# Six parameter matrices: loaded plain and transposed on TensorE, or transposed by the load itself, with another order of all operations

## The chip, the cores and the metric

The kernel runs on one core of a Trainium2 chip. TensorE (PE) multiplies matrices, VectorE (DVE) and ScalarE (ACT) work on tiles, GpSimd (POOL) does small work and adds in transfers, SyncE (SP) mostly issues transfers (DMA). The metric is the device time of one execution in microseconds (us), the median of several runs.

## The reference, cut to what matters

The input is normalised, then an S4 state space convolution and a gated feed-forward layer are applied to it, and both are added to the input.

```python
L, D, N, F = 2048, 512, 128, 1792
def _A_ref(u, A_re, A_im, B_re, B_im, C_re, C_im, log_dt, Dskip):
    dt = jnp.exp(log_dt)[:, None]
    A, Bc, Cc = A_re + 1j * A_im, B_re + 1j * B_im, C_re + 1j * C_im   # each (512, 128)
    logdA, dB = dt * A, dt * Bc
    P = jnp.exp(logdA[:, :, None] * l[None, None, :])                  # l = 0 .. 2047
    K = jnp.einsum("dn,dnl,dn->dl", Cc, P, dB).real                    # (512, 2048)
    # y = causal convolution of u with K along the sequence, through FFTs of length 4096
    return y + u * Dskip

def _B_ref(x, w_gate, w_up, w_down):
    h = sigmoid(x @ w_gate) * (x @ w_up)
    return h @ w_down

xn = layernorm(A_u)
return A_u + _A_ref(xn, ...) + _B_ref(xn, w_gate, w_up, w_down)
```

The kernel builds K from powers of exp(dt A), which VectorE and ScalarE make by a ladder of squarings and products; TensorE does the transforms and the feed-forward layer.

## The kernel before: the parts concerned

Every operation is added to a plan, `pl.add(engine, cost, function, what it needs, ...)`, and numbered in order of adding. A list of numbers, `ORDER`, says in what order the operations are written into the program; each engine runs its own in that order. The waits between engines come from a tracker that looks at which parts of which tile an instruction reads and writes. Transfers take eight semaphores in turn, so that a transfer also waits for the one eight places before it. The costs are the planner's estimates and do nothing on the chip.

```python
# loads; names are those of the plan, "Are" is the real part of A
for qi, (nm, src) in enumerate([("Are", A_A_re), ("Aim", A_A_im), ("Bre", A_B_re), ("Bim", A_B_im),
                                ("Cre", A_C_re), ("Cim", A_C_im)]):
    rawn[nm] = at(OFF["G"] + qi * KB, [D])
    l_par[nm] = load("SP", rawn[nm], src.rearrange("(p k) n -> p (k n)", k=KT), 128 * KB, pkt=1024)
    if qi == 1:
        l_ld = load("SP", ld, A_log_dt.partition_broadcast(128), 128 * KB, pkt=1024)
        l_id = load("SP", ident[:], cten["ident"].ap(), 32 * KB)
# ... w_gate in three pieces, w_up in two, x in five, w_down in one

def keep_warm(n, prio):                       # idle matmuls, results unused
    def fn():
        for _ in range(n):
            T.matmul(bank(wsl), glu_sb[:, 0, 0:128], glu_sb[:, 0, :], start=True, stop=True)
    return pl.add("PE", 0.2155 * n, fn, (), prio, acq=[wsl], rel=[wsl])
warm = [keep_warm(n, -10) for n in (12, 8, 8)]
for n in range(3):
    keep_warm(5, -9 + n)

# layernorm of x, then xn to xnT: the first 512 rows by TensorE (line 573) and ScalarE (line 578),
# the others through DRAM with Y.dma_start_transpose (line 586)

# parameters: transposed on TensorE into PSUM (line 598) and read from there with a permutation
for nm in "ABC":
    def fp(nm=nm):
        for c in range(2):
            for t in range(4):
                T.transpose(bankb(tsl[nm])[:, 512 * c + 128 * t:512 * c + 128 * t + 128],
                            rawn[nm + ("re", "im")[c]][:, 128 * t:128 * t + 128], ident[:])
    pt_op[nm] = [pl.add("PE", 0.6, fp, [l_par[nm + "re"], l_par[nm + "im"], l_id], 5, acq=[tsl[nm]])]
def raw(nm, c):
    return bankb(tsl[nm])[:, 512 * c:512 * c + 512].rearrange("p (k q) -> p q k", k=KT)
# dt = exp(log_dt) on ScalarE (line 622), z = dt * A on VectorE (line 624), range reduction,
# exp and sin on ScalarE (lines 629 to 641), then the ladder of powers (lines 674 to 688)

# gate and up projection of a group of 512 rows: TensorE (lines 1034, 1049) into PSUM banks;
# sigmoid on ScalarE (line 1043); the product on VectorE (line 1064), reading the up projection
# from PSUM, or, for the units named in UEV, from a copy that ScalarE makes (line 1060)

# spectrum: for each of two halves p of the channels and eight groups u, matmuls of lines 903, 921
# and 944, evictions of lines 908, 923 and 948, and a store of 256 KB to v_scr[p]

# last transform: v comes back in eight loads of 256 KB for each half p
vall = at(0, [NP, 8, 2, 2, DW])               # [p, t, j, r, 256], 16 KB in each partition for each p
for t in range(8):
    for p in range(NP):
        lds.append(dma("SP" if p == 0 or t % 2 == 0 else "ACT", vall[:, p, t], v_v[:, :, 2 * t:2 * t + 2, :], ...))

def s2_mm(t, r, o, start, ps=(0, 1)):         # lines 1002 and 1004; row i = 2 t + r
    for j in range(2):
        T.matmul(o[:, w], s2[:, j, :], vall[:, ps[0]:ps[-1] + 1, t, j, r, :], ...)
    if i >= 12:
        T.matmul(o[:, w], sr[:, i - 12, :], rr[:, w], ...)
# for t = 0 .. 5 the result goes to VectorE (line 1017), is added and stored as 256 KB of the output;
# rows 12 to 15 (t = 6 and 7) come on top of the down projection of the last group (lines 1082, 1099)
```

Of the kernel before, what the change touches and what calls it, by code (L numbers as in the profile page):

```python
# [14 lines left out]
ALU = mybir.AluOpType  # L15
# [160 lines left out]
def _consts():  # L176
# [30 lines left out]
UEV = (15, 17, 19, 23, 24, 25, 28, 30, 32, 33, 34, 35, 36, 37, 38, 39, 41, 42, 47)  # L207
ON_ACT = (0, 2)
ORDER = [
    1, 0, 3, 2, 39, 40, 5, 4, 23, 26, 8, 30, 29, 52, 41, 42, 31, 43, 33, 49, 32, 53, 55, 54, 57, 44, 56, 45, 46, 34, 25, 24,  # L210
    47, 6, 9, 14, 12, 19, 10, 35, 58, 36, 37, 125, 98, 59, 100, 48, 97, 7, 38, 142, 649, 63, 650, 651, 99, 65, 11, 15, 660,
    17, 637, 638, 51, 64, 113, 661, 112, 126, 66, 643, 101, 639, 67, 68, 50, 644, 645, 102, 103, 60, 680, 136, 681, 69, 655,
    656, 70, 690, 61, 691, 700, 701, 20, 13, 16, 665, 124, 104, 666, 695, 696, 685, 705, 670, 105, 686, 706, 137, 123, 671,
    702, 71, 62, 127, 662, 682, 683, 703, 663, 106, 138, 111, 72, 704, 110, 107, 108, 128, 697, 664, 148, 646, 115, 143,
    684, 698, 109, 707, 699, 129, 114, 74, 647, 708, 709, 648, 73, 640, 151, 692, 75, 693, 672, 641, 149, 76, 232, 185, 673,
    642, 77, 687, 27, 674, 694, 233, 116, 186, 675, 78, 79, 132, 676, 688, 145, 652, 677, 80, 689, 234, 187, 22, 150, 678,
    82, 144, 21, 81, 130, 667, 152, 668, 188, 679, 18, 146, 653, 654, 669, 83, 786, 657, 788, 178, 84, 658, 659, 85, 147,
    153, 787, 235, 86, 88, 710, 120, 711, 789, 791, 154, 87, 179, 792, 155, 793, 712, 156, 180, 236, 189, 190, 756, 139,
    191, 237, 89, 790, 90, 91, 713, 238, 92, 93, 118, 794, 140, 192, 95, 194, 184, 141, 172, 718, 766, 163, 173, 195, 133,
    719, 795, 203, 204, 181, 205, 197, 117, 174, 182, 198, 196, 193, 207, 720, 206, 208, 209, 211, 183, 761, 767, 757, 212,  # L220
    131, 762, 169, 726, 768, 728, 727, 170, 213, 160, 164, 214, 729, 215, 134, 200, 769, 119, 730, 770, 736, 746, 748, 216,
    166, 171, 737, 219, 749, 747, 165, 771, 121, 758, 210, 217, 750, 759, 167, 763, 772, 161, 218, 764, 220, 221, 760, 168,
    162, 765, 175, 738, 222, 94, 741, 753, 157, 201, 199, 96, 739, 176, 202, 158, 740, 778, 742, 779, 721, 223, 224, 122,
    135, 225, 239, 754, 227, 242, 751, 240, 250, 251, 244, 752, 776, 252, 159, 177, 733, 249, 254, 243, 755, 777, 255, 253,
    731, 780, 734, 245, 256, 743, 781, 258, 744, 259, 745, 782, 260, 732, 226, 773, 854, 783, 735, 247, 774, 228, 279, 722,
    241, 261, 407, 377, 775, 784, 262, 852, 378, 785, 229, 379, 280, 263, 281, 266, 230, 264, 855, 853, 437, 231, 265, 246,
    248, 268, 796, 938, 408, 376, 380, 383, 438, 267, 797, 257, 269, 282, 439, 409, 270, 798, 283, 271, 799, 284, 272, 413,
    273, 274, 275, 326, 856, 285, 834, 444, 443, 286, 440, 289, 276, 290, 295, 277, 297, 287, 298, 441, 384, 442, 278, 410,
    382, 804, 299, 301, 445, 844, 300, 302, 800, 288, 305, 327, 303, 306, 381, 411, 414, 474, 412, 446, 447, 328, 385, 805,
    386, 448, 387, 806, 449, 296, 392, 291, 292, 845, 835, 939, 294, 307, 450, 415, 388, 416, 308, 842, 417, 393, 843, 389,  # L230
    812, 832, 309, 310, 394, 399, 418, 833, 313, 390, 311, 314, 451, 467, 400, 857, 401, 312, 419, 315, 858, 329, 395, 396,
    452, 398, 397, 504, 836, 330, 316, 468, 304, 317, 469, 420, 459, 470, 473, 421, 824, 862, 475, 813, 825, 331, 453, 837,
    318, 822, 454, 293, 472, 471, 457, 489, 319, 476, 456, 863, 321, 320, 823, 838, 336, 846, 402, 332, 458, 455, 403, 333,
    864, 404, 322, 341, 344, 477, 460, 337, 807, 865, 866, 345, 478, 859, 867, 405, 461, 826, 348, 462, 346, 860, 422, 423,
    391, 479, 429, 482, 839, 349, 943, 424, 428, 426, 425, 868, 480, 347, 944, 840, 352, 872, 817, 350, 861, 463, 353, 351,
    714, 339, 338, 427, 483, 354, 869, 430, 484, 818, 342, 431, 340, 406, 512, 847, 464, 848, 870, 488, 465, 490, 432, 871,
    355, 491, 873, 356, 485, 487, 877, 433, 827, 513, 486, 514, 878, 879, 323, 434, 564, 481, 497, 324, 828, 435, 814, 829,
    492, 357, 493, 358, 494, 815, 466, 360, 830, 841, 557, 436, 516, 519, 359, 334, 362, 363, 361, 880, 849, 874, 343, 875,
    495, 881, 498, 364, 496, 325, 850, 819, 365, 518, 808, 335, 558, 499, 820, 559, 366, 367, 816, 368, 876, 821, 831, 851,
    900, 502, 515, 517, 369, 370, 371, 882, 372, 505, 560, 503, 621, 563, 501, 520, 883, 506, 884, 629, 562, 500, 561, 631,  # L240
    901, 521, 507, 885, 579, 549, 508, 509, 565, 510, 522, 602, 890, 566, 603, 523, 524, 604, 940, 542, 609, 373, 374, 511,
    941, 891, 898, 543, 567, 525, 568, 572, 550, 928, 544, 551, 610, 942, 903, 569, 611, 573, 607, 605, 570, 574, 892, 899,
    929, 904, 606, 608, 580, 612, 958, 933, 613, 526, 547, 594, 581, 545, 546, 548, 534, 614, 527, 552, 528, 553, 893, 959,
    633, 576, 578, 587, 908, 945, 529, 615, 577, 535, 946, 909, 934, 588, 589, 536, 575, 582, 947, 571, 918, 948, 949, 554,
    919, 583, 584, 635, 905, 920, 555, 906, 907, 533, 595, 530, 531, 616, 532, 585, 596, 537, 375, 894, 921, 922, 925, 963,
    953, 926, 590, 538, 964, 591, 593, 592, 597, 598, 902, 539, 886, 599, 954, 556, 586, 923, 540, 913, 617, 935, 627, 623,
    600, 541, 936, 924, 914, 601, 625, 968, 955, 956, 960, 618, 937, 957, 626, 961, 915, 962, 624, 916, 917, 930, 910, 622,
    911, 931, 965, 932, 912, 950, 619, 634, 951, 632, 927, 636, 966, 620, 967, 952, 969, 801, 723, 724, 972, 802, 725, 973,
    970, 803, 715, 628, 630, 971, 895, 974, 716, 975, 976, 809, 977, 896, 717, 887, 810, 888, 897, 980, 978, 889, 811, 981,
    982, 979, 983, 984, 985, 28, 986]  # L250
# [60 lines left out]
def kernel(  # L311
# [39 lines left out]
    def bankb(slot):  # L351
        return bank(slot).bitcast(BF)
# [88 lines left out]
    for qi, (nm, src) in enumerate([("Are", A_A_re), ("Aim", A_A_im), ("Bre", A_B_re), ("Bim", A_B_im),  # L441
                                    ("Cre", A_C_re), ("Cim", A_C_im)]):
        rawn[nm] = at(OFF["G"] + qi * KB, [D])
        lp[0] += 0.01
        l_par[nm] = load("SP", rawn[nm], src.rearrange("(p k) n -> p (k n)", k=KT), 128 * KB, pkt=1024)
        if qi == 1:
            ld = at(OFF["G"] + 6 * KB, [D])
            l_ld = load("SP", ld, A_log_dt.partition_broadcast(128), 128 * KB, pkt=1024)
            l_id = load("SP", ident[:], cten["ident"].ap(), 32 * KB)
# [82 lines left out]
    warm = [keep_warm(n, -10) for n in (12, 8, 8)]  # L532
# [59 lines left out]
    tsl = {nm: _Slot(b) for nm, b in (("A", "gu"), ("B", "gu"), ("C", "po"))}  # L592
    pt_op = {}
    for nm in "ABC":
        def fp(nm=nm):
            for c in range(2):
                for t in range(4):
                    T.transpose(bankb(tsl[nm])[:, 512 * c + 128 * t:512 * c + 128 * t + 128],
                                rawn[nm + ("re", "im")[c]][:, 128 * t:128 * t + 128], ident[:])
        pt_op[nm] = [pl.add("PE", 0.6, fp, [l_par[nm + "re"], l_par[nm + "im"], l_id], 5, acq=[tsl[nm]])]  # L600

    def raw(nm, c):
        return bankb(tsl[nm])[:, 512 * c:512 * c + 512].rearrange("p (k q) -> p q k", k=KT)
# [16 lines left out]
    perm = lambda v: v.rearrange("p (q k) -> p q k", k=KT)  # L620
# [5 lines left out]
    q1 = pl.add("DVE", 0.60, lambda: tt(perm(pt_["z_im"]), raw("A", 1), perm(dtb), ALU.mult), [o_dt] + pt_op["A"], PR)  # L626
    q2 = pl.add("DVE", 0.60, lambda: tt(perm(pt_["z_re"]), raw("A", 0), perm(dtb), ALU.mult), [q1], PR, rel=[tsl["A"]])
# [24 lines left out]
    def f_g():  # L652
        tt(perm(pt_["db_re"]), raw("B", 0), perm(dtb), ALU.mult)
        tt(perm(pt_["db_im"]), raw("B", 1), perm(dtb), ALU.mult)
    qb = pl.add("DVE", 1.27, f_g, [o_dt] + pt_op["B"], PR + 2, rel=[tsl["B"]])

    def f_g2():
        tt(perm(pt_["t1"]), raw("C", 0), perm(pt_["db_re"]), ALU.mult)
# [494 lines left out]
```

## Time and profile before

| | |
|---|---|
| Time, median of 3 runs | 246.35 us (246.32 to 246.81) |
| Span of the profiled execution | 244.9 us |
| TensorE busy | 230.0 us (94%), 2070 matmuls in the records |
| VectorE busy | 187.6 us (77%) |
| ScalarE busy | 180.4 us (74%) |
| Idle matmuls (line 529) | 43, 11.9 us |
| Transposes of the parameters (line 598) | 24, in three groups of 0.61 us |
| Moved by DMA | 43.60 MB, mean 178 GB/s |

The profile is one execution in time. Busy shares are averages over the whole span, and this kernel has stages with different limits, so it is read stage by stage: which engine is full, and which wait ends last. In the lines shown further down, L12 is line 12 of the kernel, "big" is one large tile that holds most of the buffers, x8 is the number of instructions, and brackets name the idle time before an instruction and what ended it. "PEclk" or the clock in a table of stages is the granted clock of TensorE, 1.00 at full speed.

### The profile page before, as it was taken

The page shows a single profiled execution, that of the slowest core. Times are in us where ns is not written, and L with a number is a line of the kernel's source. Part 1 is how long each engine was busy: PE and PEld are TensorE (multiplying, and loading weights), DVE is VectorE, ACT ScalarE, POOL GpSimd, SP SyncE. Part 2 cuts the span into 40 slices and gives each one's busy share as a digit, 9 for nine tenths or more (in the row PEclk, how much of TensorE's full clock was granted, in tenths as well). Part 3 has the DMA queues.
Part 4 walks back from the last instruction along what each step waited for, and adds up shares of the span by engine and source line. Part 5 has one row for each costly group of instructions (what it writes and reads, how often), then busy time and mean ns, then how long its engine had stood idle before and what let it go on. Part 6 is the DMA issues. An engine that isn't in the chain of part 4 may idle for free.

```text
span 244.9 us, 5395 instructions
## 1 busy us (share of the span) xinstructions
PE 230.0 (94%) x2070; PEld 116.8 (48%) x2098; DVE 187.6 (77%) x397; ACT 180.4 (74%) x293; POOL 17.4 (7%) x42
## 2 busy tenths in 40 slices
PE   7959999899999999999999999999999999987695
PEld 2526444344444644555556555465555454433242
DVE  3899999999999999999999999923415345816232
ACT  5899999999999999659899999945577877000000
POOL 1202350000000200120000200000000200000000
PEclk9979999999999999999999999999999999999589
DMA  6999537122256964298376867636958987843403
GB/s 170 302 376 357 208 119 183 60 86 86 87 188 202 250 135 139 82 210 231 88 212 187 212 157 223 178 88 188 287 139 231 191 231 222 237 152 120 155 24 129
DMA packets 48459, 43.60 MB, mean 178 GB/s; under 512 B 9393, under 2 KB 41650, under 8 KB 48434
## 3 DMA queue, kind: packets, MB, share of 16 engines
q1 hardware_dynamic: 46338, 40.58, 55.9%
q0 software_dynamic: 864, 1.57, 4.1%
q10 hardware_dynamic: 1232, 1.11, 1.5%
q8 instruction: 16, 0.26, 0.5%
q14 instruction: 9, 0.07, 0.1%
HBM read 25.43 MB, written 12.06 MB: 153 GB/s over the span
## 4 chain that ended last, share of the span: by engine, by line
PE 41%; ACT 37%; DMA 9%; DVE 6%; issue 4%; SPq 1%; ACTq 0%
PE bank L1082 13%; PE bank L1034 6%; ACT hT_sb L1043 6%; PE pair L921 5%; DMA big<-v_scr 5%; ACT big L674 5%; PE bank L1049 4%; ACT big L705 4%; PE pair L828 3%; PE pair L944 3%; ACT big L557 3%; ACT sq_sb L796 3%; ACT big L680 2%; PE pair L1002 2%; ACT big L948 2%
## 5 line engine op out<-in xcount | busy, mean ns | idle before, releaser
L1034 PE MATMUL bank<-xnT,wg_sb 128*128 128x512 bf16 (+1 forms) x227 | 55.4, 377 | 2.3 <-ACT xnT L578 0.5
L1049 PE MATMUL bank<-xnT,wu_sb 128*128 128x512 bf16 x218 | 53.0, 379 | 1.0 <-issue 0.3
L1082 PE MATMUL bank<-wd_sb,hT_sb 128*128 128x512 bf16 x215 | 51.7, 389 | 1.1 <-issue 0.5
L1034 PEld LDWEIGHTS <-wg_sb 128*128 128x128 bf16 x236 | 23.0, 100 | 27.0 <-issue 5.1
L1082 PEld LDWEIGHTS <-hT_sb 128*128 128x128 bf16 x224 | 22.1, 100 | 27.5 <-issue 4.2
L1043 ACT ACTIVATE hT_sb<-bank 128x512 bf16<-128x512 f32 x56 | 32.8, 612 | 1.5 <-PE bank L1034 1.5
L1049 PEld LDWEIGHTS <-wu_sb 128*128 128x128 bf16 x224 | 20.9, 98 | 25.6 <-issue 2.5
L927 DVE TENSOR_TENSOR big<-big 128x2048 bf16<-128x2048 bf16 x16 | 19.5, 1216 | 17.8 <-DMA big<-big 11.2
L1064 DVE TENSOR_TENSOR hT_sb<-hT_sb,bank 128x512 bf16<-128x512 bf16 x37 | 24.3, 682 | 6.5 <-PE bank L1049 6.1
L739 DVE TENSOR_TENSOR big<-big 128x1024 bf16<-128x1024 bf16 (+4 forms) x40 | 25.7, 643 | 0.4
L740 DVE TENSOR_TENSOR big<-big 128x1024 bf16<-128x1024 bf16 (+4 forms) x40 | 25.7, 641 | 0.0
L921 PE MATMUL pair<-big 128*128 128x256 bf16 x160 | 20.0, 273 | 0.0
L908 ACT ACTIVATE big<-pair 128x1024 bf16<-128x1024 f32 x16 | 16.5, 1035 | 4.2 <-DMA big<-c_SR 2.3
L923 ACT ACTIVATE big<-pair 128x1024 bf16<-128x1024 f32 x16 | 16.4, 1026 | 3.2 <-PE pair L921 2.1
L948 ACT ACTIVATE big<-pair 128x1024 bf16<-128x1024 f32 x16 | 16.5, 1037 | 2.5 <-DMA v_scr<-big 1.4
L921 PEld LDWEIGHTS <-big 128*128 128x128 bf16 x160 | 15.3, 98 | 4.8 <-issue 1.0
L744 DVE TENSOR_TENSOR big<-big 128x512 bf16<-128x512 bf16 (+4 forms) x40 | 16.8, 419 | 0.2
L745 DVE TENSOR_TENSOR big<-big 128x512 bf16<-128x512 bf16 (+4 forms) x40 | 16.7, 417 | 0.0
L705 ACT ACTIVATE big<-pair 128x1024 bf16<-128x1024 f32 x16 | 16.3, 1042 | 0.0
L796 ACT ACTIVATE sq_sb<-big 128x256 bf16<-128x256 bf16 (+2 forms) x20 | 12.9, 650 | 2.5 <-DVE big L745 2.4
L674 ACT ACTIVATE big<-big 128x512 bf16<-128x512 f32 x24 | 13.9, 637 | 0.0
L529 PE MATMUL bank<-glu_sb 128*128 128x512 bf16 x43 | 11.9, 433 | 1.4 <-POOL glu_sb L522 1.4
(109 smaller groups left out, 276.8 us busy)
## 6 DMA issues: line engine op xcount, KB each, us to landing
big<-c_E SPq DMA_DIRECT2D x16, 320.0 KB, 3.9
z_scr<-big SPq DMA_DIRECT2D x16, 256.0 KB, 2.5
big<-z_scr SPq DMA_DIRECT2D x16, 256.0 KB, 3.6
big<-big SPq DMA_DIRECT2D x64, 64.0 KB, 3.1
v_scr<-big SPq DMA_DIRECT2D x16, 256.0 KB, 3.0
big<-v_scr SPq DMA_DIRECT2D x12, 256.0 KB, 4.3
big<-in_A_u_dram SPq DMA_DIRECT2D x4, 512.0 KB, 5.5
wd_sb<-in_B_w_down_dram SPq DMA_DIRECT2D x1, 1792.0 KB, 14.3
```

The costliest lines, as they stand in the source:

```text
L674: S.activation(out=W[p][:, k], in_=cur[:, :, DW * p:DW * p + DW], func=ACT.Identity)
L705: ev = pl.add("ACT", 0.90, lambda sl=sl, zs=zs: S.activation(out=zs().rearrange("p j d -> p (j d)"), in_=two(sl), func=ACT.Identity), [fx_ ...
L739: V.tensor_tensor(out=wide(outp), in0=wide(lo), in1=mre, op=ALU.mult)
L740: V.tensor_tensor(out=wide(tb()), in0=wide(lo), in1=mim, op=ALU.mult)
L796: a = pl.add("ACT", 0.11 + 0.213 * nn, lambda: S.activation(out=sq().rearrange("p r k c h -> p r k (c h)"), in_=src.rearrange("p r k c h - ...
L921: T.matmul(two(sk)[:, o:o + DW], es()[:, g, kt, :], kT[p][:, kt, :], start=kt in (0, NKT - 1), stop=kt >= NKT - 2)
L948: ev = pl.add("ACT", 0.90, lambda sv=sv, vs=vs: S.activation(out=vs().rearrange("p g y d -> p (g y d)"), in_=two(sv), func=ACT.Identity), ...
L1034: T.matmul(bank(sl)[:, c0:c1], w[:, kt, k * 128:(k + 1) * 128], xnT[:, grp, kt, c0:c1], start=(kt == 0), stop=(kt == KT - 1))
L1043: S.activation(out=hT_sb[:, hs.idx, k % 2, :], in_=bank(sl), func=ACT.Sigmoid)
L1049: T.matmul(bank(sl), wu_sb[:, kt, k * 128:(k + 1) * 128], xnT[:, grp, kt, :], start=(kt == 0), stop=(kt == KT - 1))
L1064: V.tensor_tensor(out=h(), in0=h(), in1=us_sb[:, us.idx, :] if on else bank(sl), op=ALU.mult)
L1082: T.matmul(bank(po), hT_sb[:, hts[k // 2].idx, k % 2, jj * 128:(jj + 1) * 128], wd_sb[:, k, :], start=(k == 0), stop=k == FT - 1, **kw)
```

## The change

The six parameter matrices, each 512 x 128 and 128 KB, are no longer loaded in plain form, transposed on TensorE and read from PSUM with a permutation. Each load transposes, the matrices land in SBUF in the form that the products need, and VectorE reads them there. This is meant to free TensorE and two PSUM banks early in the kernel and to leave the products without a permutation. The idle matmuls of the start, three blocks of 12, 8 and 8, become one of 28. Last, the order of all operations is another one, made with slack for transfers that come late, and another set of up projections (20 instead of 19) is copied by ScalarE.

```diff
-UEV = (15, 17, 19, 23, 24, 25, 28, 30, 32, 33, 34, 35, 36, 37, 38, 39, 41, 42, 47)
+UEV = (18, 19, 27, 28, 29, 30, 31, 32, 33, 34, 35, 36, 37, 38, 39, 40, 41, 44, 45, 52)
 ORDER = [          # cut to its end
-    ... 617, 935, 627, 623, 600, 541, 936, 924, 914, 601, 625, 968, 955, 956, 960, 618, 937, 957, 626, 961,
-    915, 962, 624, 916, 917, 930, 910, 622, 911, 931, 965, 932, 912, 950, 619, 634, 951, 632, 927, 636, 966,
-    620, 967, 952, 969, 801, 723, 724, 972, 802, 725, 973, 970, 803, 715, 628, 630, 971, 895, 974, 716, 975,
-    976, 809, 977, 896, 717, 887, 810, 888, 897, 980, 978, 889, 811, 981, 982, 979, 983, 984, 985, 28, 986]
+    ... 613, 936, 627, 629, 617, 947, 907, 932, 960, 937, 952, 614, 961, 619, 962, 964, 890, 623, 615, 891,
+    967, 965, 710, 625, 892, 711, 966, 631, 712, 621, 968, 969, 804, 718, 805, 971, 719, 806, 970, 972, 882,
+    883, 796, 975, 720, 797, 884, 798, 973, 976, 978, 974, 979, 977, 980, 981]
@@ loads of the six matrices
-        l_par[nm] = load("SP", rawn[nm], src.rearrange("(p k) n -> p (k n)", k=KT), 128 * KB, pkt=1024)
+        l_par[nm] = pl.add("SP", 1.27, lambda src=src, dst=rawn[nm]: Y.dma_start_transpose(dst, src), (), lp[0] + ...,
+                           dma=(128 * KB, _rate(256), 0.5))
@@ idle matmuls
-    warm = [keep_warm(n, -10) for n in (12, 8, 8)]
+    warm = [keep_warm(28, -10)]
@@ parameters
-    tsl = {nm: _Slot(b) for nm, b in (("A", "gu"), ("B", "gu"), ("C", "po"))}
-    for nm in "ABC":
-        def fp(nm=nm): ...                    # eight transposes on TensorE, as above
-        pt_op[nm] = [pl.add("PE", 0.6, fp, [l_par[nm + "re"], l_par[nm + "im"], l_id], 5, acq=[tsl[nm]])]
+    pt_op = {nm: [l_par[nm + "re"], l_par[nm + "im"]] for nm in "ABC"}
     def raw(nm, c):
-        return bankb(tsl[nm])[:, 512 * c:512 * c + 512].rearrange("p (k q) -> p q k", k=KT)
+        return rawn[nm + ("re", "im")[c]]
@@ the eight products with the parameters, one of them
-    q1 = pl.add("DVE", 0.60, lambda: tt(perm(pt_["z_im"]), raw("A", 1), perm(dtb), ALU.mult), [o_dt] + pt_op["A"], PR)
+    q1 = pl.add("DVE", 0.60, lambda: tt(pt_["z_im"], raw("A", 1), dtb, ALU.mult), [o_dt] + pt_op["A"], PR)
```

Five operations fewer are added, so a number above 46 after the change means the operation that was five higher before. The two ends, read with the names of the operations:

| | before | after |
|---|---|---|
| SyncE at first | x, x, A im, A re, identity, log_dt, C re, B re, C im, x, S1, x, w_gate 1, B im, w_gate 2, w_gate 3, x, w_down, w_up 1, w_up 2 | x, x, log_dt, A re, A im, identity, S1, x, w_gate 1, B im, B re, x, w_gate 3, x, w_gate 2, C re, SW, C im, Dskip, w_up 2, w_up 1, two stores of z, w_down |
| TensorE at first | 12 + 5 idle, transposes of A, 8 + 8 idle, transposes of xn, S1, gate units 2, 4, 0, transposes of C, gate 1, transposes of B, ... | 28 + 5 + 5 idle, transposes of xn, 5 idle, S1, gate units 2, 0, 10, S1, gate units 12, 8, 9, ... |
| Five idle matmuls | one group in the middle of the first group of rows, one after the last matmul | none there |
| Gate and up groups after the last product of half 1 | ten | seven |
| The end, on all engines | loads of half 1 for t=2, 1, 0, 6, 5, 7; down product of row 12; t=2; t=1; down product of row 13; row 13; row 12; t=0; loads of half 1 for t=3 and t=4; t=5; ... | loads of half 1 for t=5, 6, 0, 1; down product of row 12; t=5; load for t=3; down product of row 13; row 12; t=0; load for t=4; store of t=5; load for t=7; store of t=0; load for t=2; row 13; t=3; t=1; ... |

## The prediction

> **What bounds the kernel now.** I read the page first, then a table of busy time by stage, then the first 24 us in order of time, then the chain of waits from 200 us on and what the queue of SyncE waited for there. The span is 244.9 us. By stage (columns: stretch, length, busy time and instructions of PE, weight loads, DVE, ACT, POOL, granted clock, DMA share, GB/s):
>
> ```profile
> 15.00:30.00 15.00, 14.04 (x80) 7.74 (x81) 14.30 (x32) 14.94 (x27) 4.06 (x6) 0.89 0.92 317
> 130.00:150.00 20.00, 19.68 (x263) 11.13 (x266) 19.98 (x38) 19.55 (x35) 1.24 (x3) 1.00 0.70 175
> 150.00:205.00 55.00, 54.27 (x661) 29.63 (x668) 28.23 (x48) 39.12 (x54) 2.28 (x3) 1.00 0.75 202
> 205.00:218.00 13.00, 12.28 (x64) 5.34 (x65) 6.41 (x15) 2.87 (x5) 0.00 (x0) 1.00 0.74 223
> 218.00:230.00 12.00, 8.77 (x37) 3.64 (x38) 4.78 (x5) 0.00 (x0) 0.00 (x0) 0.88 0.40 135
> ```
>
> From 15 to 150 us TensorE, VectorE and, but for a stretch around 100, ScalarE are all busy; from 150 to 205 TensorE alone is full (54.27 of 55). So a stage gives time back only at the two ends. The start, in order of time:
>
> ```profile
> 3.08 0.43 SPq L417 DMA_DIRECT2D big<-in_A_log_dt_dram  x1
> 7.75 1.29 DVE L624 TENSOR_TENSOR big<-bank,big 128x512 f32<-128x512 bf16 x2
> 13.48 1.92 ACT L578 ACTIVATE xnT<-pair 128x1024 bf16<-128x1024 bf16 x2
> 14.54 0.38 PE L703 MATMUL pair<-big 128*128 128x512 bf16 x1 [2.14 <-ACT xnT L578]
> 15.45 4.45 PE L1034 MATMUL bank<-xnT,wg_sb 128*128 128x256 bf16 x20 [0.54 <-ACT xnT L578]
> ```
>
> The chain is: log_dt lands (7.1), exp, dt times A on VectorE (7.75), range reduction, exp and sin on ScalarE until 13.48, only then the eviction of the transposed xn, and the first gate matmul at 15.45. TensorE, whose last transposes ended at 12.39, stood still for 2.1 us, and the granted clock was 0.50 from 16 to 18 us.
>
> The end, first the chain, then a wait of SyncE's queue:
>
> ```profile
> 209.31 8.71 DMA big<-v_scr
> 218.03 1.89 PE pair L1002 x8
> 219.92 3.02 PE bank L1082 x14
> ...
> 224.05 4.20 DMA big<-v_scr
> 228.30 1.89 PE pair L1002 x4
> 230.19 1.71 PE bank L1082 x4
> ```
>
> ```profile
> SPq L417 <- PE bank L1004: 1.4, 1, 1.4
> ```
>
> Six of the eight loads of the second half of v arrive by 218.0. The last two (t=3, t=4) are issued at 224.05, just as the matmuls of row 12 end: in the program they wait for these. The reason is the shape of the read. `vall[:, 0:2, t, j, r, :]` takes 512 bytes from the first half and 512 bytes 16 KB further on; the program's dependency tracking treats everything between as read, so loads for other t, listed later, wait for it, and reads listed after those loads wait for them. TensorE stood 3.2 us (225.1 to 228.3) and the clock was then 0.50 until 234. A matmul of 512 columns starts every 0.43 us there and every 0.216 us before, so some 14 matmuls cost about 2.9 us more.
>
> **What the Trainium skill says.** "TensorE: Matmul & The Clock Gate", section "Why this matters for your kernels", advises no PE-idle gaps over about 3 us between matmul bursts, or the clock falls to half. The trace agrees in kind, and here gaps of 2.1 us (start) and 3.2 us (end) were followed by 0.50, while 0.6 us at 217.4 was not. "Advanced Engine Details and Errata", section "X-Bar Transpose (TRN2)", says that transposing DMAs are as fast as regular ones. In landing, about: the three of 512 KB took 4.4 to 5.4 us, plain loads of 512 KB took 5.5 (median). In issuing, no:
>
> ```profile
> L586 SPq DMA_TRANSPOSE xnT<-x_scr x3: 2080/2225/2520, 37.4 to 80.2; - x3
> ```
>
> against 0.43 us for a plain load. "VectorE: DVE Perf Modes", section "Why PSUM operands drop a tier", says that fp32 with a PSUM operand runs at 1x. The eight products here take 0.683 us with PSUM input and fp32 output; products of fp32 in SBUF (line 648) take 0.66, so I expect almost nothing from the move to SBUF.
>
> **The change part by part.**
> 1. TensorE loses 24 transposes of the parameters. Eight ended at 7.6 us, in idle time; the other 16 lie between 19.6 and 21.2 us and cost 2 x 0.61 = 1.2 us of a full engine.
> 2. The idle matmuls stay 43. Before, one group of five runs inside the full stretch (5 x 0.216 = 1.1 us), and five come after the last real matmul. After, 28 + 5 + 5 run at first and five right behind the transposes of xn. That takes 1.1 us out of the full stretch. From 1.43 us on, 17 matmuls took 5.75 us before; 21 more at 0.216 bring after's first 38 to about 11.7 us, just when xn is ready; the last five then cover one of the two idle microseconds, so the half clock after 15.45 may go: seven starts of 0.43 against 0.216, up to 1.6 us.
> 3. The start of the chain. log_dt is issued third, at about 1.65 instead of 3.08, and with its 4.0 us lands near 5.6. The two A transposes follow it. I estimate 1.1 us of issue each (the trace's 2.2 for four times the size, of which part must be fixed), so the second is issued by 4.3 and lands 2.2 to 2.9 us later, near 6.9. The product can start about 0.8 us sooner than 7.75, and the first gate matmul with it, near 14.7. It is not certain: ScalarE now does exp between two rows of statistics.
> 4. The four B and C transposes hold SyncE's queue 4 x (1.1 - 0.43) = 2.7 us longer ahead of weights and x. w_down (1.75 MB) however goes behind both w_up, which takes about 5 us of transfers (at 350 GB/s) out of their way. After's third gate unit already needs the last piece of w_gate, two units sooner than I would like, near 17 us: a stall up to 1 us.
> 5. VectorE: unchanged, but for 20 instead of 19 evictions of the up projection taken over by ScalarE (0.49 us each there, 0.68 down to 0.42 here).
> 6. The order. Up to the first table product (c=0) both lists have nearly the same TensorE work ahead, and so again at c=1 to c=3. After has 3 us more of VectorE work listed ahead of c=0 and none more at c=1, so I count the middle as neutral, with 2 us of doubt.
> 7. The end. After the last product of the second half (end T; 204.8 before) after has seven gate and up groups left before the first final matmul, not ten: 7 x 0.86 + 0.75 + 3.1 = about 10.2 us of filler for a wait that took 13.2 us with six loads. After needs only four loads for t=5, 0.5 MB less, at 0.23 MB/us some 2.2 us less: ready near T + 10.9. Idle 0.7, as before. Then t=5, the down product of row 13's block (3.0), row 12 of t=6, t=0: T + 16. Now row 13 is listed behind the loads of t=4 and t=2, and overlaps both by the shape above. The load of t=4 may go when row 12 is done. The load of t=2 stands in SyncE's queue behind the store of t=0, which waits for t=0's matmuls (0.9) and its addition (1.23); then two issues (1.0) and a landing of about 3. Together 6.2 us after row 12, of which t=0 covers 0.9: TensorE idles about 5.3 us instead of 3.2. The half clock follows as before. Cost: +2.1 us.
>
> Sum: of 1.2 + 1.1 + 1.6 + 0.8 = 4.7 us at the start I count 2, since VectorE is full until 150 us and does not get shorter; late transfers +0.6; the end +2.1. That is +0.7: 246.35 + 0.7 = 247.0 us.
>
> **The rivals.**
> The start wins in full (TensorE is the bound from 150 us on, and whatever it did sooner is not left for then): -4.7 + 2.1 gives 243.7. For it speaks 54.27 of 55 us; against it VectorE's 19.98 of 20 between 130 and 150.
> The transposing loads are late: if each takes as long to issue as the large ones (2.2 us), the second A lands at about 9, the chain starts 1.3 us later than before and the weights some 7 us later, with PE waits at a half clock: 250 to 252. For it speaks that issue time hardly varies (2.08 to 2.52); against it the planner's own cost in the diff, 1.27.
> The end is better than I read: if the load of t=2 isn't tied up behind the store, the gap stays under 3 us and perhaps the clock stays full: 2 to 5 us less, 242 to 245.
> The order's slack pays: TensorE's idle time between 15 and 205 us, 4.4 us now, halves: 245.
>
> **Range and chances.** The rivals lie from 242 to 252, most of them within 3 us of 247. Two per cent is 4.9 us. Eight in ten: 243.5 to 251. Faster by over 2% (under 241.4) needs the full start and a cured end together: 0.06. Slower by over 2% (over 251.3) needs late transposes or a stall in the middle: 0.10. The rest, 0.84, within.
>
> **What would show it.** The first gate matmul near 14.7 with the clock at 1.00 shows steps 2 and 3; a DMA_TRANSPOSE of the parameters at 0.9 to 1.3 us of issue shows step 4; a wait of TensorE on v_scr of about 5 us before row 13, followed by 0.50, shows step 7. I am wrong if the first gate matmul comes after 16, if TensorE idles over 6 us between 15 and 205, or if there is no such wait at the end.

## The result, and the profile after

The kernel after takes 249.72 us (median of 4 runs, 249.01 to 250.49) where the kernel before took 246.50 beside it (4 runs, 246.32 to 246.81): a ratio of 1.013, with a 95% interval of 1.0091 to 1.0169. That is inside the predicted range, within the 2%, and 2.7 us above the predicted 247.0. So the change costs 3.2 us where 0.7 was expected, and it is the sum and not only its size that has to be explained: the start came out at least as well as predicted, the wait at the end came out as predicted, and in between something was lost.

The table by stage of the kernel after (the columns as in the prediction: stretch, length, then busy time and instructions of PE, weight loads, DVE, ACT and POOL, granted clock, DMA share, GB/s):

```profile
15.00:30.00 15.00, 13.81 (x72) 6.82 (x72) 13.66 (x33) 14.16 (x27) 4.95 (x9) 1.00 0.98 307
150.00:205.00 55.00, 52.86 (x638) 28.61 (x645) 28.13 (x48) 39.21 (x54) 2.24 (x3) 1.00 0.72 194
205.00:218.00 13.00, 11.14 (x80) 4.80 (x70) 6.79 (x16) 3.24 (x5) 0.00 (x0) 1.00 0.77 215
218.00:230.00 12.00, 5.78 (x26) 2.42 (x27) 3.05 (x3) 0.59 (x1) 0.00 (x0) 0.86 0.45 132
```

At the start the clock is 1.00 instead of 0.89. From 150 us on TensorE has holes that the kernel before does not have: 2.1 us from 150 to 205 (before 0.7), 1.9 from 205 to 218 (before 0.7), 6.2 from 218 to 230 (before 3.2). Part of what looks like a hole, in both, is a matmul without a record: there are 2070 matmuls to 2098 weight loads before and 2045 to 2074 after.

The start in order of time (start, us, engine or queue, operation; idle time before it and its releaser in brackets):

```profile
2.13 1.23 SPq L445 DMA_TRANSPOSE big<-in_A_A_re_dram  x1
...
6.45 1.30 DVE L616 TENSOR_TENSOR big<-big 128x512 f32<-128x512 bf16 x2
...
14.16 1.91 PE L1026 MATMUL bank<-xnT,wg_sb 128*128 128x256 bf16 x16 [0.32 <-ACT xnT L579]
...
17.03 0.82 PE L1026 MATMUL bank<-xnT,wg_sb 128*128 128x512 bf16 x3 [0.97 <-DMA wg_sb<-in_B_w_gate_dram]
```

A transposing load of a parameter holds SyncE's queue for 1.23 us. The first product starts at 6.45 (before 7.75) and the first gate matmul at 14.16 (before 15.45). At 17.03 TensorE has waited 0.97 us for the third piece of w_gate. The first gate matmul is not a fixed point: in e2 (further down), whose program is the same up to the end, it comes at 15.03 and TensorE doesn't wait for w_gate.

```profile
15.03 3.00 PE L1026 MATMUL bank<-xnT,wg_sb 128*128 128x256 bf16 x20
```

By 18.3 us the two are level: the next gate groups start at 18.34 in after and at 18.30 in e2.

The end, first as the chain that ended last (start, us, what), then the matmul behind its longest wait, from the view in order of time:

```profile
218.58 1.05 PE pair L994 x4
...
224.67 1.24 DVE big L1009
225.92 0.34 SPq L417
...
226.32 3.61 DMA big<-v_scr
229.96 1.01 PE bank L994 x2
```

```profile
229.96 1.01 PE L994 MATMUL bank<-big 128*128 128x512 bf16 x2 [5.39 <-DMA big<-v_scr]
```

The addition of t=0 on VectorE, then the store in SyncE's queue, then a load of v, then row 13: TensorE stands still for 5.39 us.

**Marks.** Two moments turned out to divide the span well: the start of the fourth and last table product on TensorE (call it P4; P1 is the first), and T, the end of the last product of the second half. They are read in the view in order of time (tiles of 128*32 mark a table product). P4 and T of the kernel before:

```profile
158.44 2.71 PE L828 MATMUL pair<-big 128*32 128x82 bf16 x128
...
203.32 1.49 PE L944 MATMUL pair<-big 64*64 64x512 bf16 x32
```

and of the kernel after:

```profile
160.91 2.84 PE L820 MATMUL pair<-big 128*32 128x82 bf16 x128 [0.25 <-ACT big L900]
...
205.98 1.01 PE L936 MATMUL pair<-big 64*64 64x512 bf16 x16 [0.73 <-DVE big L919]
```

Although the first gate matmul comes 1.3 us sooner, P1 comes 0.7 us later (81.8 and 82.4 in the same view) and P4 2.5 us later. T is 203.32 + 1.49 = 204.8 before and 207.0 after. Kernels with the same program up to there differ by up to 0.7 us at P1 (before, e1 and e9: 81.8, 82.3 and 82.4) and 0.6 at P4 (before and e1), so at P1 before and after can't be told apart. The same marks of every kernel that was run, each from its own profile (us; "tail" is the span less T):

| kernel | time, median | P1 | P4 | P4 to T | tail | span |
|---|---|---|---|---|---|---|
| before | 246.50 | 81.8 | 158.4 | 46.4 | 40.1 | 244.9 |
| after | 249.72 | 82.4 | 160.9 | 46.1 | 40.2 | 247.2 |
| e1: before, v by row | 240.24 | 82.3 | 159.0 | 46.4 | 33.0 | 238.4 |
| e2: after, v by row | 240.46 | 82.4 | 160.8 | 46.4 | 30.9 | 238.0 |
| e3: after's list to 140 us, then before's | 249.57 | 82.2 | 163.3 | 46.4 | 38.1 | 247.8 |
| e4: before's list to 142 us, then after's | 259.90 | 86.1 | 172.1 | 46.4 | 43.1 | 261.6 |
| e5: before, idle blocks moved | 245.41 | 82.7 | 159.4 | 46.4 | 37.8 | 243.5 |
| e6: before, transposing loads | 251.34 | 85.8 | 164.2 | 46.4 | 39.3 | 249.9 |
| e7: after, plain loads | 250.84 | 83.8 | 162.4 | 46.7 | 40.3 | 249.4 |
| e8: e2 and 20 idle matmuls | 244.96 | 82.1 | 165.1 | 46.9 | 30.8 | 242.8 |
| e9: e1 and 20 idle matmuls | 244.92 | 82.4 | 163.4 | 48.1 | 33.1 | 244.5 |
| e11: e2, two places of the list mended | 240.19 | 82.4 | 160.7 | 47.0 | 30.6 | 238.3 |
| e12: after, the same two places | 249.75 | 82.6 | 161.0 | 46.6 | 39.8 | 247.4 |
| e13: e2, less VectorE work | 240.17 | 82.4 | 161.0 | 46.0 | 31.0 | 237.9 |

Not all kernels were timed at the same moment and on the same chip; the kernel before, timed beside each of them, had medians of 245.1 to 246.5, so where a per cent matters the ratio to it is given below. The profile of e4 is of its longest execution, 263.51 us, so its marks stand only roughly beside its median.

### The profile page after: what moved, and what is told of

Same layout as the page of the kernel before. It is cut to its first block, busy times and chain, and to the rows that moved or that the text cites. A ratio compares the mean times of both kernels' runs of the same rounds, so it can differ in the third digit from the quotient of the medians.

```text
span 247.2 us, 5353 instructions
## 1 busy us (share of the span) xinstructions
PE 227.4 (92%) x2045; PEld 114.2 (46%) x2074; DVE 187.6 (76%) x397; ACT 181.6 (73%) x294; POOL 18.4 (7%) x42
## 4 chain that ended last, share of the span: by engine, by line
PE 45%; ACT 21%; DMA 17%; SPq 7%; issue 5%; DVE 4%; ACTq 0%; DVEq 0%
PE bank L1074 12%; PE bank L1026 9%; DMA big<-v_scr 6%; PE bank L1041 5%; SPq L417 5%; PE pair L913 5%; PE pair L820 4%; ACT hT_sb L1035 4%; DMA big<-z_scr 4%; ACT big L697 3%; ACT big L666 3%; DMA wd_sb<-in_B_w_down_dram 3%; DMA wg_sb<-in_B_w_gate_dram 3%; PE pair L994 3%; ACT big L672 2%
## 5 line engine op out<-in xcount | busy, mean ns | idle before, releaser
L1026 PE MATMUL bank<-xnT,wg_sb 128*128 128x512 bf16 (+1 forms) x224 | 54.4, 368 | 2.6 <-DMA wg_sb<-in_B_w_gate_dram 1.0
L1074 PE MATMUL bank<-wd_sb,hT_sb 128*128 128x512 bf16 x217 | 50.5, 379 | 0.9 <-ACT glu_sb L1104 0.3
L1026 PEld LDWEIGHTS <-wg_sb 128*128 128x128 bf16 x236 | 21.6, 98 | 26.7 <-issue 5.3
L1074 PEld LDWEIGHTS <-hT_sb 128*128 128x128 bf16 x224 | 21.4, 98 | 26.2 <-issue 1.6
L772 ACT ACTIVATE big<-big 128x256 bf16<-128x256 bf16 x32 | 13.1, 454 | 1.1 <-PE pair L820 1.1
```

Of the source, the lines that this page charges most:

```text
L1026: T.matmul(bank(sl)[:, c0:c1], w[:, kt, k * 128:(k + 1) * 128], xnT[:, grp, kt, c0:c1], start=(kt == 0), stop=(kt == KT - 1))
L1074: T.matmul(bank(po), hT_sb[:, hts[k // 2].idx, k % 2, jj * 128:(jj + 1) * 128], wd_sb[:, k, :], start=(k == 0), stop=k == FT - 1, **kw)
```

## The experiments

### The false waits at the end (e1, e2)

v is laid out by row instead of by half, so that what a final matmul reads of a row lies together, and its range no longer covers other rows. Nothing else changes; e1 is the kernel before with this edit, e2 the kernel after.

```diff
-    vall = at(0, [NP, 8, 2, 2, DW])
-    vps = [[vall[:, p, t] for t in range(8)] for p in range(NP)]
+    vall = at(0, [8, NP, 2, 2, DW])
+    vps = [[vall[:, t, p] for t in range(8)] for p in range(NP)]
 ...
-            T.matmul(o[:, w], s2[:, j, :], vall[:, ps[0]:ps[-1] + 1, t, j, r, :], ...)
+            T.matmul(o[:, w], s2[:, j, :], vall[:, t, ps[0]:ps[-1] + 1, j, r, :], ...)
```

> Kernel before, with the returned v laid out by t first (vall[t, p, ...]), so that a read of one t no longer spans the places of the others; nothing else changes. Theory (false waits between loads and reads of different t): the 3.2 us stand at 225 and the half clock after it, 2.9 us, go, and the first final matmul starts sooner: 240.5 to 242. Rival (the loads are late in any case, the shape of the read only names the wait): 245.5 to 247.

> Changed kernel with the same layout of v. Theory (false waits): the wait of 5.4 us before row 13, the half clock after it (about 3 us) and part of the 1.6 us before t=5 go: 240 to 243, about the same as the kernel before with this layout or up to 1.5 us off it. Rival (loads late in any case): 247 or more.

Measured: e1 240.24 us (ratio to before 0.9777, 0.9726 to 0.9829), just under the range of the theory, e2 240.46 (0.9796, 0.9738 to 0.9853), inside it. By the ratios the false waits cost the kernel before 2.2% of 246, 5.5 us, and the kernel after 1.3 + 2.0 = 3.3%, 8.2 us; cured of them the two are equal. So 2.7 us of the 3.2 are made by those waits, and 0.5 or less by all the rest together, though the rest was to be a gain. (Each ratio is known to 0.4 to 0.6%, so the 2.7 may be off by over 1 us.) By stage, e1 and then e2:

```profile
160.00:205.00 45.00, 45.00 (x496) 24.65 (x488) 18.83 (x25) 29.65 (x40) 1.76 (x2) 1.00 0.75 198
205.00:218.00 13.00, 13.00 (x80) 5.81 (x73) 6.40 (x15) 3.40 (x5) 0.00 (x0) 1.00 0.82 254
```

```profile
160.00:205.00 45.00, 43.57 (x513) 24.20 (x512) 17.89 (x26) 30.93 (x41) 2.25 (x3) 1.00 0.74 199
205.00:218.00 13.00, 11.90 (x75) 5.30 (x75) 6.91 (x16) 3.72 (x5) 0.00 (x0) 1.00 0.83 231
```

The order of before keeps TensorE without a hole from 160 to 218 us; the order of after leaves 1.4 + 1.1 = 2.5 us of holes there, with the false waits gone. The tail is 2.1 us shorter in e2 (30.9 to 33.0), since three gate and up groups fewer are left for it, and P4 is 1.8 us later: the two cancel. P1 and P4 in e1 and then in e2, each followed by the stretch from P4 to T in the table by stage:

```profile
82.26 2.70 PE L828 MATMUL pair<-big 128*32 128x82 bf16 x128 [0.19 <-ACT big L780]
...
158.99 2.70 PE L828 MATMUL pair<-big 128*32 128x82 bf16 x128
...
158.99:205.35 46.36, 46.36 (x545) 25.81 (x542) 19.84 (x27) 30.89 (x40) 1.76 (x2) 1.00 0.74 197
```

```profile
82.42 2.70 PE L820 MATMUL pair<-big 128*32 128x82 bf16 x128 [0.39 <-ACT big L772]
...
160.76 2.84 PE L820 MATMUL pair<-big 128*32 128x82 bf16 x128 [0.25 <-ACT big L900]
...
160.76:207.11 46.35, 44.07 (x527) 24.61 (x528) 19.28 (x26) 31.20 (x41) 2.25 (x3) 1.00 0.73 194
```

In e1 TensorE is busy for all of the 46.36 us from P4 to T; in e2 it stands still for 2.3 us of them.

### One list up to the middle, the other from there (e3, e4)

Both have the code of after; the set of up projections that ScalarE copies follows the mixed list (18 in e3, 23 in e4). e3 takes after's list up to about 140 us and then what is left in before's order (with two pairs of gate and up units of the last row group exchanged, so that the two lists fit); e4 takes before's list up to about 142 us and then after's.

```diff
 # e3
-ORDER = [ after's ]
+ORDER = [ after's, up to and with 478 ] + [ what is left, in before's order ]
 # e4
+ORDER = [ before's, up to and with 428 ] + [ what is left, in after's order ]
```

> Changed kernel (transposing loads, idle matmuls first, its list up to the last spectrum input of the first half, about 140 us), and from there on the list of the kernel before. In the list of before two pairs of gate and up units of the last group change names so that the buffers fit. Theory 1 (the start of the changed kernel is worth about 4 us of TensorE work, and its own list of the second half loses them again): 246.5 - 3.7, so 241.5 to 244. Theory 2 (from 150 us on the chain of products and transfers sets the pace and a lead of TensorE only turns into waiting): 245.5 to 247.5.

> The other way round: transposing loads too, but the list of the kernel before up to about 142 us, and then that of the changed kernel. Theory 1 (the second half of the changed list loses 4.4 us, its end 2.1 more, whatever came first): 252 to 255. Theory 2 (its second half is bound by its own chain, a later start of it costs little): 249 to 250.5.

Measured: e3 249.57 us (ratio 1.0126, 1.0037 to 1.0214), e4 259.90 (1.0566, 1.0497 to 1.0634). Neither theory had it. In e3 the joint itself loses:

```profile
150.00:160.00 10.00, 6.41 (x108) 3.53 (x109) 9.99 (x17) 6.58 (x12) 0.00 (x0) 0.66 0.51 138
```

TensorE is busy for 6.41 of 10 us right behind the joint, and P4 slips to 163.3. In e4 P1 is already 4.3 us later than in the kernel before, which e6 explains below. As tests of the two ends they are inconclusive. One thing of theirs could be used afterwards: P4 to T took 46.4 us in both, as in the kernel before.

### Parts of the start (e5, e6, e7)

e5 is the kernel before with the idle matmuls moved as the change moves them, in the list alone:

```diff
-... 25, 24, 47, ... 36, 37, 125, ... 687, 27, 674, ... 985, 28, 986
+... 25, 24, 28, 47, ... 36, 37, 27, 125, ... 687, 674, ... 985, 986
```

> The kernel before, with only the idle matmuls moved as the change moves them: 28 + 8 at first, five right behind the transposes of xn; none in the full stretch. Theory 1 (a lead of TensorE at the start is spent before the end): TensorE is some 2 to 2.7 us ahead of the kernel before at 25 us of the span (1.1 us of idle matmuls less, and no half clock after 15.5 us), and the time stays within 0.7 us of the kernel before, 245.3 to 246.7. Theory 2 (a lead counts in full, as TensorE is full from 130 to 205 us): 243.2 to 244.6.

Measured: 245.41 us, ratio 1.0009 (0.9983 to 1.0036): nothing. But theory 1 is right only in the time, not in its reason: there is no lead to be spent. P1 comes at 82.7, later than the 81.8 of before and the 82.3 of e1, whose program is the same up to the end. The stretch of e5 that was to gain:

```profile
15.00:30.00 15.00, 12.40 (x77) 6.86 (x77) 14.32 (x32) 14.43 (x25) 3.24 (x5) 1.00 0.93 321
```

The half clock is gone (1.00, before 0.89) and so are five idle matmuls, and TensorE is then idle for 2.6 us instead of 1.0: it waits for ScalarE's evictions, which were the next limit here.

e6 puts the transposing loads into the order of before, with the idle matmuls as 28 at first; e7 puts the plain loads and the transposes on TensorE into the order of after:

```diff
 # e6, against before
-            T.transpose(...)                      # 24 of them, and plain loads
+    l_par[nm] = ... Y.dma_start_transpose(dst, src)
 # e7, against after: the same lines the other way round,
 # with A's transposes ahead of the first product, B's and C's behind those of xn
```

> The kernel before's order of the rest, with the parameters loaded by transposing loads in place of plain loads and 24 transposes on TensorE, and the idle matmuls as 28 at first. If what the transposing loads save (1.2 us of TensorE, an earlier first product) counts as in step 1 of the prediction: 244.5 to 246. If in this order they hold up SyncE's queue ahead of the weights, so that the start is 2.5 to 3.5 us behind, as it was in the run with the end of after: 248 to 250.

> The kernel after's order, with the parameters loaded plainly and transposed on TensorE as in the kernel before. Theory 1 (the lead at the start is spent before the end; the whole loss is made at the end by loads that wait for each other): 249 to 250.7, as the kernel after, though TensorE is 1 to 2.5 us behind it at 25 us. Theory 2 (the lead counts): 251 to 253. A third way: the transposing loads hold up SyncE's queue more than they save, and the time falls to 247.5 to 248.9.

Measured: e6 251.34 us (ratio 1.0259, 1.0211 to 1.0307), e7 250.84 (1.0262, 1.0199 to 1.0324). e6 is worse than either expectation: P1 is 3.5 us later than in e1 and P4 5.2 us. The first gate matmul comes at 17.53, 2.2 us later than in e1 (15.34). TensorE's waits from 15 to 60 us (total, times, longest) name the weights, which stand behind the transposing loads in SyncE's queue, for 1.6 + 0.6 us, as in the prediction's second rival:

```profile
PE bank L1018 <- ACT hT_sb L1027: 2.1, 5, 0.5
PE bank L1018 <- DMA wg_sb<-in_B_w_gate_dram: 1.6, 1, 1.6
PE bank L1033 <- DMA wu_sb<-in_B_w_up_dram: 0.6, 1, 0.6
```

Where the rest of the 5.2 us is lost was not traced. In the order of after the same loads are worth something: e7, without them, and with the transposes and the idle blocks of before in their place, has P1 1.4 us later than after, P4 1.5 later, and the span is 2.2 us longer. e7's time lies between the two theories; the marks decide for the second: with one and the same list, what TensorE gains at the start is still there at P4 and at the end.

### What sets the pace up to P4 (e8, e9, e13)

Twenty idle matmuls (4.3 us of TensorE) near 140 us, in e2 (e8) and e1 (e9):

```diff
+    def idle_later():
+        for _ in range(20):
+            T.matmul(bank(wd), wg_sb[:, 0, 0:128], wg_sb[:, 0, 0:512], start=True, stop=True)
+    pl.add("PE", 0.2155 * 20, idle_later, (), 50, acq=[wd], rel=[wd])   # listed near 140 us
```

> The kernel after with v laid out by row (no false waits at the end, 240.46), and 20 idle matmuls (4.3 us of TensorE) added near 140 us, where it is some 4 to 5 us ahead of the kernel before in the same layout. Theory 1 (the lead is slack that the second half doesn't use): 240.2 to 241.8. Theory 2 (TensorE sets the pace from 140 us on): 244.2 to 245.2.

> The kernel before with v laid out by row (240.24) and the same 20 idle matmuls near 140 us. It has no lead there and its TensorE is busy for 54.8 of 55 us from 150 to 205, so both theories say 243.8 to 244.8. If it is less than 242, TensorE is not what sets the second half in this kernel either.

Measured: e8 244.96 us (ratio 1.0007, 0.9988 to 1.0027), e9 244.92 (1.0011, 0.9988 to 1.0034); against e2 and e1 that is 2.1% and 2.3% by the ratios and 4.5 and 4.7 us by the medians, the 4.3 in full and a little more (e9 is 0.1 above the range expected). P4 moves by 4.3 in e8 and 4.4 in e9. So between P3 and P4 TensorE has no slack in either kernel; the stretches ahead of P3 were not tested in this way. Theory 1, that after's lead is slack, falls as I had put it. VectorE was held up too by these matmuls (7.40 us busy from 150 to 160 in e8, 9.96 in e2), so this pair alone does not rule VectorE out; e13 does. It is e2 with less work on VectorE: in the complex products of the fourth table product one multiplication and both additions run over half of the columns, so part of the table is left uncombined.

```diff
+        R = NPR // 2 if less[0] else NPR          # less[0] = c == 3
-            V.tensor_tensor(out=wide(tb()), in0=wide(lo), in1=mim, op=ALU.mult)
+            V.tensor_tensor(out=wide(tb())[:, 0:R], in0=wide(lo)[:, 0:R], in1=mim[:, 0:R], op=ALU.mult)
-            V.tensor_tensor(out=outp[:, :, :, 0, :], ...)      # and the same for component 1
+            V.tensor_tensor(out=outp[:, 0:R, :, 0, :], ...)
```

> The kernel after with v laid out by row (240.46), with VectorE's work in the fourth table product cut: one of the two multiplications and both additions of each complex product run over half of the columns, some 6 us less of VectorE between 120 and 160 us; nothing else changes. Theory 1 (VectorE, full to 160 us and no sooner done than in the kernel before, holds the second half, and TensorE's lead of 4.9 us at 160 us waits for it): TensorE spends its lead, and the time falls by 2 to 3.5 us, to 237 to 238.5. Theory 2 (TensorE and the transfers behind it set the pace, whatever VectorE does): 239.8 to 240.8.

Measured: 240.17 us (ratio 0.9801, 0.9748 to 0.9854): no change. The stage concerned in e13 (in e2 VectorE was busy for 29.96 us of it):

```profile
130.00:160.00 30.00, 29.59 (x401) 15.14 (x400) 26.50 (x63) 27.04 (x45) 3.28 (x8) 1.00 0.64 173
```

VectorE loses 3.5 us of this stretch (4.5 in the whole span, less than the 6 I had reckoned), and P4 stays at 161.0, T at 207.0. Theory 2: VectorE, at 29.96 of 30, is full and not the bound.

### Mending two waits of after's list (e11, e12)

A gate group goes ahead of the M2 product (line 895) that waited for its reload of z, and a gate and an up group go ahead of the product of line 936 that waited for VectorE, which the expectation calls the table multiplication (the three evictions between them move along).

```diff
-955, 927, 568, 540, 543, 541, 918
+955, 927, 918, 568, 540, 543, 541
 ...
-938, 940, 948, 549, 578, 596, 579, 939, 949, 941, 889, 370, 881, 942, 550, 958, 915
+938, 940, 948, 549, 578, 596, 939, 949, 941, 958, 915, 579, 889, 370, 881, 942, 550
```

> The kernel after with v laid out by row (240.46, span 238.0), and two places of its list mended: a gate group moved ahead of the M2 product that waited 0.9 us for its reload of z, and a gate and an up group moved ahead of the table multiplication that waited 1.1 us for VectorE. Theory 1 (TensorE sets the pace all the way, so its lead from the start is lost in waits of after's own list in the second half; 2.5 us of them from 160 to 218 us): the two waits go and the time falls to 238.2 to 239.4. Theory 2 (the second half is tied to VectorE and the transfers, and waits only move): 240.0 to 241.

> The same two moves in the kernel after as it is (249.72). Theory 1: 247.5 to 248.5, as the last loads are issued after the matmuls they falsely wait for, and those come sooner. Theory 2: 249.2 to 250.5; the end then waits longer for the same loads, whatever TensorE gained before.

Measured: e11 240.19 us (0.9816, 0.9773 to 0.9860), e12 249.75 (1.0195, 1.0141 to 1.0249, where after had 1.0130). Theory 2 in both: nothing gained. TensorE's waits from 190 us on, in e2 and then in e11:

```profile
PE pair L936 <- DVE big L919: 1.1, 1, 1.1
PE pair L895 <- DMA big<-z_scr: 0.9, 1, 0.9
```

```profile
PE pair L986 <- DMA big<-v_scr: 0.9, 1, 0.9
...
PE pair L928 <- DVE big L911: 0.5, 1, 0.5
PE pair L887 <- DMA big<-z_scr: 0.4, 1, 0.4
```

The two waits of 2.0 us are down to 0.9, but T is 0.6 us later, as two groups now stand ahead of it, and a wait of 0.9 for v has come up behind. The waits moved.

## Why the prediction was right and wrong, by its steps

**Steps 1 and 3, the start: right.** The chain starts 1.3 us sooner than before (6.45), where I had 0.8; the first gate matmul comes at 14.16, where I had 14.7, and at 15.03 in e2; the issue of a transposing load, estimated at 1.1 us, took 1.23. e7 measures transposing loads against plain ones in after's order: 1.4 to 1.5 us at P1 and at P4.

**Step 2, the idle matmuls: half right.** The half clock after 15.45 is gone. But in before's order the move brings nothing (e5), because ScalarE's evictions come next: there the 1.1 + 1.6 us could not be added to the rest. In after's order the start gained about 4.2 us by the count under step 6, of which e7 ascribes 1.4 to the loads and the transposes that they save; how the idle matmuls and the order share the other 2.8 no run shows.

**Step 4: right in place and size in the profile of after (0.97 us at 17.03),** but not a loss by itself: e2, whose program is the same there, comes 0.9 us later to its first gate matmul, has no such wait and is level with after at 18.3 us. That these loads can hurt much more under another order, e6 shows.

**Step 5: right.** VectorE's busy time is 187.60 us before and 187.65 after.

**Step 6: this is the step that failed.** I wrote that up to each table product "both lists have nearly the same TensorE work ahead" and counted the middle as neutral. Counting gate, up and down groups ahead of each mark in the two lists (a gate or up group is four matmuls of 512 columns, 0.86 us; a down group fourteen, 3.0 us) gives something else:

| ahead of | before: gate, up, down | after: gate, up, down | more in after |
|---|---|---|---|
| P1 | 24, 24, 4 | 27, 26, 4 | 5 x 0.86 = 4.3 us |
| P2 | 30, 29, 6 | 30, 29, 7 | 3.0 us |
| P3 | 37, 32, 8 | 39, 35, 8 | 5 x 0.86 = 4.3 us |
| P4 | 44, 42, 8 | 45, 44, 9 | 3 x 0.86 + 3.0 = 5.6 us |
| T | 54, 48, 12 | 54, 51, 12 | 3 x 0.86 = 2.6 us |

After's order puts its gain at the start into groups ahead of the table products. With 4.3 us more ahead of P1 and P1 at the same time (82.3 in e1, 82.4 in e2), the start gained about 4.2 us; with 5.6 more ahead of P4 and P4 1.8 later, 3.8 of it are still there at P4; at T, with 2.6 more ahead and T 1.8 later, only 0.8. So of the 4.7 us that I had summed, some 4 were real and lasted to P4, and 3 of them went between P4 and T. My reason to count only 2, "since VectorE is full until 150 us and does not get shorter", was wrong as well: e13 takes VectorE work out of the stretch from 130 to 160 and no mark moves, and e8 and e9 show TensorE's time counting in full from P3 on. What the gain bought was not time. From P4 to T takes 46.0 to 47.0 us in all the runs but e9 (48.1), whatever came before. There the order of before has one down group (3.0 us) more to lay beside the chain of z and v than the order of after, and after stands still for 2.3 us in its place (e2). Three groups fewer are left for the tail, which is 2.1 us shorter once the false waits are cured. Start, middle and tail together: 240.24 to 240.46, nothing, where I had -2 + 0.6.

**Step 7, the end: right in mechanism and nearly in size.** I said that TensorE would idle about 5.3 us before row 13, behind the load of t=2, that load behind the store of t=0, that store behind its addition. It idled 5.39, along that chain, and half clock followed. Between the profiles, the tails give what the false waits cost: 40.1 - 33.0 = 7.1 us before, 40.2 - 30.9 = 9.3 after, so +2.2 for the predicted +2.1; the ratios of the timed runs give 5.5 and 8.2, +2.7, with more doubt. That the tail itself is shorter I had seen (seven groups, not ten), but had not taken into the sum, since I kept T at one and the same time.

Sum: predicted -2 + 0.6 + 2.1 = 0.7; measured about 0.5 + 2.7 = 3.2. Most of the miss, 1.9 us of the 2.5, is step 6, and 0.6 the end. That it missed by no more is luck: two wrong terms worked against each other. With the start counted at its real 4.2 us and the middle still as neutral, the sum would have been -4.2 + 0.6 + 2.1 = -1.5, 4.7 us off.

**The rivals.** "The start wins in full" was right in that the gain lasts to P4, and wrong in the time for the reason of step 6. "The end is better than I read" and "the order's slack pays" did not come: from 15 to 205 us TensorE's holes grew from 4.4 to 6.1 us (the table by stage, with 97.58 of 100 busy from 30 to 130 and 19.64 of 20 from 130 to 150), just over the 6 that I had named as a sign of being wrong. In e1 and e2, whose programs are the same there, and where every weight load has its matmul, they are 2.7 and 3.2 us; in neither pair did they halve. "The transposing loads are late" came true only in before's order (e6).

**What stays open.** Why P4 to T takes 46 us in after's order is not settled. In before's order it is TensorE's own work, which fills it in e1; e2 has 3 us less work there, stands still for 2.3 us and is no faster; VectorE between 130 and 160 us (e13) and the two largest waits alone (e11) are not what holds it. The reloads of z and the loads of v through the queue of SyncE are left, and were not tested by themselves. An order that keeps after's start but lists three groups less ahead of P4 should move P4, and with it T, forward, if the 46 us hold; it was not tried. Of the versions that compute the whole, e1, e2 and e11 are the fastest, 2.2, 2.0 and 1.8% below the kernel before.

## To carry to other kernels

When an order is changed, count the work that each list puts ahead of every mark of the chain (here the four table products) before counting what a stage gains: a gain on the engine that is the bound is only time if the work that ends the kernel comes sooner, and this one was spent on filler that is needed later, beside waits. An engine that is busy 29.96 of 30 us need not be the bound; take some work off it and see whether a mark moves. And lay a buffer out so that what one instruction reads is contiguous: a strided read that spans other rows made loads and matmuls wait for each other here, and curing it was worth more than the whole change.

## What the runs showed of the hardware

Of the six transposing loads of a 512x128 bf16 parameter in after, five held SyncE's queue for 1.13 to 1.25 us (the sixth, C re, for 2.95; why is not shown). A plain load of log_dt held it for 0.43, and the transposing loads of x in before, with four times the size, for 2.08 to 2.52: a quarter of the size took about half of the time.

The clock: after, with a hole of 5.39 us, has 0.86 from 218 to 230; e2, in which TensorE has no hole over 1.13 us behind its first gate matmul, has 1.00 from 15 us to the end. The Trainium skill, "TensorE: Matmul & The Clock Gate", section "Why this matters for your kernels", advises against gaps over about 3 us; these two runs agree. Shorter holes close together can be too much as well: at the start of before, 2.14 us and, one matmul later, 0.54 us were followed by 0.50. A single hole of that size in e4 was not, and the clock there is 1.00 from 207 to 214:

```profile
209.36 0.41 PE L887 MATMUL pair<-big,m 64*64 64x512 bf16 x4 [2.12 <-DMA big<-z_scr]
```

The clock column has to be read with care at the very start: in e2 it shows 1.00 from 0 to 7 us, though the idle matmuls start only every 0.43 us until then, twice the 0.216 of later ones.

That the first products read SBUF instead of PSUM changed nothing: 1.29 us for two before, 1.30 after.
